# A fused attention and two-layer feed-forward kernel: order of weight preparation, place of the result sums, and where the first quad's products stand

## The chip, the core and the metric

The kernel runs on one core of a Trainium2 chip. The time is device microseconds of one execution, the median of several; smaller is better. Engines are called by their names or as the profile abbreviates them: TensorE (PE, its weight loads PEld), VectorE (DVE), ScalarE (ACT), GpSimd (POOL) and SyncE (SP), which issues nearly all DMAs.

## The reference

```python
# q, k, v: (4, 8, 576, 64), s: (4, 8, 576)
cum  = cumsum(maximum(s, 0), -1)
bias = -(cum[..., :, None] - cum[..., None, :])
scores = where(causal, -1e9, scale * q @ k.T + minimum(bias, 0))
x = (softmax(scores) @ v), heads joined             # (2304, 512)
h = x @ moe_w_in;   g = maximum(0.01 * h, h)         # 512 -> 2048
x = g @ moe_w_out                                    # 2048 -> 512
h = x @ moe2_w_in;  g = maximum(h, 0) + log1p(exp(-abs(h)))
out = g @ moe2_w_out                                 # (2304, 512)
```

The weights arrive as 64-bit floats.

## The kernel before

**Numbers in two parts.** Every matmul operand is a pair of rounded tiles, high and low, and each product is three matmuls (high by high, high by low, low by high). ScalarE rounds a tile to its high part, GpSimd (or VectorE) subtracts to get the low part.

**Stages.** Attention ends near 247 us. The first feed-forward layer goes through 68 steps: four groups of four blocks of 128 hidden units, in a group the token chunks (512, 512, 256, 512, 512 tokens; two of 384 in the first group), for each chunk the four blocks. Step n issues `h_mm` (12 matmuls) for itself and, `LAG` = 3 steps late, `out_mm(n-3)` (12 matmuls). At the fourth block of a chunk VectorE adds four PSUM banks to `acc` (L861). Five banks take turns for these sums, so the next chunk's first `out_mm` needs the adds of the last chunk. ScalarE makes `gf` (`leaky`, L834), and a step later `g_parts` makes `gh` on ScalarE and `gl` on GpSimd (L151).

**Weights on the way.** A block of 64-bit weights is loaded raw by SyncE (`load_w`, L93 for the first matrix, L98 for the second; 512 KB) into one of two raw buffers, one step before ScalarE reads it. `split_w` turns a block of the first layer into a pair: Abs and Copy on ScalarE, four steps on VectorE (L114, L117, L120, and the integer add L123), Copy on ScalarE, subtraction on GpSimd (L133). `prepare` does the same for the 32 blocks of the second layer, adds the sums of quarter blocks that a seven-product block scheme (Strassen-Winograd) needs, and `stage` (L705) writes high and low parts back to DRAM as `w2d`: the two `move`s (L713, L714) stand next to each other in SyncE's queue, and the second one needs GpSimd's result. `at(n, ...)` puts work into step n, `later(n, ...)` into a tick n steps on, `plan` holds it. Each engine works its queue strictly in the order in which the code issues.

**Second layer.** 16 quads (2 pairs of token chunks, 8 double blocks). A quad's seven products go into four banks X, Y, K, Z (L1026); VectorE adds the products into results in SBUF (`join`, L1038); for each of four results a `Unit` computes maximum(h, 0) + log1p(exp(-abs(h))): four ACT steps, `value` (L978) and `rest` (L981) on VectorE, `correct` (L984) and `low` (L992) on GpSimd. Then eight output sums (L1075) that VectorE adds to `acc` (L1081 for the first, L1083). The 256 tokens between the pairs go the plain way (`Plain`, L1102). `on(t, ...)` gives every piece a time; pieces are issued in order of these times, about 1.36 us of TensorE to a unit. The operands `B11`, `T1` to `T4`, `B21`, `B22` of the quads are sums of quarters of `acc` (`combine`, `x_high`, `x_low`).

## Time and profile before

| what | us |
|---|---|
| median of 3 runs | 975.86 (974.29 to 975.87) |
| the profiled execution, its own time | 974.51 |
| span in its profile | 972.7 |
| busy: TensorE | 952.0 (98%) |
| busy: VectorE, ScalarE, GpSimd | 714.9, 576.6, 532.2 |

The page divides the span into the busy time of each engine; matmuls overlap, so the busy sum of TensorE says little on gaps. Those are read from the starts of consecutive matmuls in the timeline, and from the view of waits, which says which instruction released a waiting one.

### The profile page before, as it was taken

How to read it: one execution, taken by the hardware profiler on the slowest of the kernel's cores; microseconds unless marked ns; L12 is line 12 of the kernel's file. 1: busy time of each engine (PE TensorE's matmuls, PEld its weight loads, DVE VectorE, ACT ScalarE, POOL GpSimd, SP SyncE). 2: the span in 40 equal slices, each digit the busy share in tenths (PEclk: the TensorE clock that was granted, in tenths of full speed). 3: DMA queues.
4: the chain of work that ended last, by engine and by line, in shares of the span. 5: the costliest groups of instructions: out<-in, count | busy, mean ns of one | idle time of the engine just before them, and what ended most of it. 6: DMA issues, size and time to landing. Idle time of an engine off the chain costs nothing.

```text
span 972.7 us, 15423 instructions
## 1 busy us (share of the span) xinstructions
PE 952.0 (98%) x5173; PEld 767.4 (79%) x5173; DVE 714.9 (73%) x1326; ACT 576.6 (59%) x1185; POOL 532.2 (55%) x516
## 2 busy tenths in 40 slices
PE   9999999999999989998999999999999999999998
PEld 6666777777988868886888888788888778888786
DVE  7888667553368778996877725787779887887777
ACT  6888667564565455555554525765566675555562
POOL 7788556452356576756755422755445454555443
PEclk9999999999999999999999999999999999999999
DMA  7444442411636566556686133242425248345302
GB/s 243 143 160 145 128 144 98 149 61 47 227 105 218 168 192 206 186 185 201 197 272 232 49 130 130 92 133 74 160 64 172 87 144 309 132 134 170 131 0 87
DMA packets 79251, 143.61 MB, mean 148 GB/s; under 512 B 7626, under 2 KB 24906, under 8 KB 79172
## 3 DMA queue, kind: packets, MB, share of 16 engines
q1 hardware_dynamic: 78740, 141.87, 44.3%
q8 instruction: 41, 0.67, 0.3%
q10 hardware_dynamic: 432, 0.75, 0.2%
q14 instruction: 38, 0.31, 0.1%
HBM read 109.33 MB, written 33.25 MB: 147 GB/s over the span
## 4 chain that ended last, share of the span: by engine, by line
PE 69%; DVE 8%; POOL 7%; issue 5%; DMA 5%; ACT 5%; SPq 1%; POOLq 0%; DVEq 0%; ACTq 0%
PE ps_out L1075 15%; PE ps_h L145 13%; PE ps_h L1026 13%; PE ps_out L854 9%; PE pt_s L316 4%; PE pt_t L377 3%; PE ps_o L635 3%; PE pt_v L409 3%; PE ps_h L1102 2%; DMA rawi<-in_moe_w_in 2%; POOL stg L712 2%; DMA rawo<-in_moe_w_out 2%; POOL l L984 1%; PE pt_s L409 1%; POOL gl L992 1%
## 5 line engine op out<-in xcount | busy, mean ns | idle before, releaser
L984 POOL TENSOR_TENSOR l<-l,v 128x512 f32<-128x512 f32 x72 | 94.6, 1314 | 140.0 <-DVE v L981 134.9
L151 POOL TENSOR_TENSOR gl<-gf,gh 128x512 fp32r<-128x512 f32 (+2 forms) x68 | 91.1, 1341 | 115.3 <-ACT gh L150 65.9
L360 POOL TENSOR_SCALAR sc<-sc,st 128x512 f32<-128x512 f32 (+4 forms) x160 | 88.4, 563 | 79.3 <-DVE st L356 61.5
L992 POOL TENSOR_TENSOR gl<-l,gh 128x512 fp32r<-128x512 f32 x72 | 95.3, 1324 | 53.6 <-ACT gh L988 53.6
L145 PE MATMUL ps_h<-xh,wih 128*128 128x512 f32 (+2 forms) x320 | 120.4, 376 | 0.0
L145 PE MATMUL ps_h<-xl,wih 128*128 128x512 f32 (+2 forms) x320 | 118.4, 370 | 0.0
L145 PE MATMUL ps_h<-xh,wil 128*128 128x512 f32 (+2 forms) x320 | 118.3, 370 | 0.0
L1075 PE MATMUL ps_out<-woh,gh 128*128 128x512 f32 x290 | 113.4, 391 | 2.2 <-DVE acc L1081 1.4
L1075 PE MATMUL ps_out<-wol,gh 128*128 128x512 f32 x290 | 112.5, 388 | 0.0
L988 ACT ACTIVATE gh<-l 128x512 fp32r<-128x512 f32 x72 | 45.6, 633 | 108.6 <-POOL l L984 108.4
L854 PE MATMUL ps_out<-gh,woh 128*128 128x512 f32 (+2 forms) x272 | 100.6, 370 | 6.5 <-DVE acc L861 6.5
L349 ACT ACTIVATE sc<-sc,st 128x512 f32<-128x512 f32 (+2 forms) x144 | 83.4, 581 | 34.7 <-DVE st L337 28.8
L854 PE MATMUL ps_out<-gl,woh 128*128 128x512 f32 (+2 forms) x272 | 100.1, 368 | 2.2 <-POOL gl L151 2.2
L1083 DVE TENSOR_TENSOR acc<-ps_out,acc 128x512 f32<-128x512 f32 (+1 forms) x127 | 85.6, 678 | 19.8 <-PE ps_out L1075 18.8
L854 PE MATMUL ps_out<-gh,wol 128*128 128x512 f32 (+2 forms) x272 | 99.9, 367 | 0.0
L1026 PE MATMUL ps_h<-xh,wih 128*128 128x512 f32 x224 | 89.1, 398 | 0.8 <-DVE u L1038 0.7
L1075 PE MATMUL ps_out<-woh,gl 128*128 128x512 f32 x290 | 88.9, 388 | 0.0
L1038 DVE TENSOR_TENSOR u<-ps_h,u 128x512 f32<-128x512 f32 x80 | 55.1, 688 | 44.3 <-PE ps_h L1026 30.8
L1026 PE MATMUL ps_h<-xl,wih 128*128 128x512 f32 x224 | 87.4, 390 | 0.0
L1026 PE MATMUL ps_h<-xh,wil 128*128 128x512 f32 x224 | 87.2, 389 | 0.0
L834 ACT ACTIVATE gf<-ps_h 128x512 f32<-128x512 f32 (+2 forms) x68 | 36.7, 540 | 62.7 <-PE ps_h L145 52.8
L981 DVE SCALAR_TENSOR_TENSOR v<-v,e 128x512 f32<-128x512 f32 x72 | 73.7, 1024 | 0.0
(169 smaller groups left out, 2361.9 us busy)
## 6 DMA issues: line engine op xcount, KB each, us to landing
w2d<-stg SPq DMA_DIRECT2D x88, 256.0 KB
rawi<-in_moe_w_in SPq DMA_DIRECT2D x32, 512.0 KB
rawo<-in_moe_w_out SPq DMA_DIRECT2D x32, 512.0 KB
wih<-w2d SPq DMA_DIRECT2D x64, 256.0 KB
wil<-w2d SPq DMA_DIRECT2D x64, 256.0 KB
woh<-w2d SPq DMA_DIRECT2D x32, 256.0 KB
wol<-w2d SPq DMA_DIRECT2D x32, 256.0 KB
K<-in_k SPq DMA_DIRECT2D x15, 432.0 KB
```

The source lines that it names most:

```text
L145: nc.tensor.matmul(ps, a, b, start=kk == 0 and n == 0, stop=kk == KD - 1 and n == 2)
L151: nc.gpsimd.tensor_tensor(gl, gf, gh.bitcast(F32), op=ALU.subtract)
L349: nc.scalar.activation(x, x, AF.Exp, scale=-1.0, bias=self.stat(0, e + self.last), accum_out=self.stat(1, e))
L360: nc.gpsimd.tensor_scalar(x, x, self.stat(2, e), 1.0, op0=ALU.mult, op1=ALU.mult)
L854: nc.tensor.matmul(ps, a, b, start=f == 0 and m == 0, stop=f == G - 1 and m == 2)
L981: nc.vector.scalar_tensor_tensor(self.t, self.t, -1.0, self.e, op0=ALU.add, op1=ALU.subtract)
L984: nc.gpsimd.tensor_tensor(self.l, self.l, self.t, op=ALU.subtract)
L992: nc.gpsimd.tensor_tensor(self.gl, self.l, self.gh.bitcast(F32), op=ALU.subtract)
L1026: nc.tensor.matmul(self.ps[name], x, y, start=n < 4 and kp == 0 and m == 0, stop=kp == 1 and m == 2, skip_group_check=n >= 4,)
L1038: nc.vector.tensor_tensor(self.u[out], self.ps[bank], self.u[other], op=ALU.add)
L1075: nc.tensor.matmul(u, a, v, start=m == 0, stop=m == len(ops) - 1)
L1083: nc.vector.tensor_tensor(d[..., w], o[..., w], d[..., w], op=ALU.add)
```

## The change

The change has three parts, and SBUF moves between them.

1. **Preparation of weights.** The second weight pool is gone until the second layer (six buffers of each kind instead of eight). Raw buffers are four instead of two, and a raw block is loaded two steps ahead. All 32 `prepare` blocks use one ring of four `ws` tiles, `stage` has six `stg` buffers instead of four. 22 of the 32 blocks are spread over groups 1 and 2, ten over the first 13 steps of group 3. The move of the low part is issued one tick after that of the high part. The add for second-matrix blocks of the first layer goes from VectorE to GpSimd. `g_parts` goes to the front of its tick.
2. **Sums in PSUM.** Joins write into the banks Y, K and Z themselves, e + 1 goes into one PSUM bank `v` (a tile in SBUF for the first quad), and `rest` writes over e. Z is one bank for all quads. Units start every 2.6 instead of 2.1 units of time, `high` and `low` come later in them. T1 and T2 overwrite B11 in `acc`, and some `x_low` go to GpSimd.
3. **First quad.** Its seven products are issued before the last three `out_mm` of the first layer, its operands are made over more steps, and its first-matrix weights are fetched at step 18 of the last group.

```diff
 def split_w(layer, f, nm, at):
-        wp = wpools[(layer * NF + f) % (2 * G) // 6]
+        wp = wpools[0]
         def add():
-            wio.get("add", nc.gpsimd).tensor_tensor(m, m, t, op=ALU.add)
+            wio["add"][nm].tensor_tensor(m, m, t, op=ALU.add)
...
-    wio["i"] = wio["o"] = enter(0, "raw", bufs=2)
-    wio["add"] = nc.vector
+    wio["i"] = wio["o"] = enter(0, "raw", bufs=4)
+    wio["add"] = {"i": nc.vector, "o": nc.gpsimd}
...
 def stage(j, k, src, own=False):
-        hi = tpool.tile([P, DM], F32R, tag="stg", name="stg", bufs=4)
+        hi = prep.tile([P, DM], F32R, tag="stg", name="stg", bufs=6)
...
             move(w2d[j, k], hi)
-            move(w2d[j, k + 1], lo)
+            later(1, move, w2d[j, k + 1], lo)
...
 def prepare(n, j, e, nm):
-        if nm == "i":
-            m = tpool.tile([P, DM], I32, tag="ws", name="ws", bufs=2)
-        else:
-            m = wio["tmp"].tile([P, DM], I32, tag="wm", name="wm")
+        m = prep.tile([P, DM], I32, tag="ws", name="ws", bufs=4)
...
 def leaky(n, N, ps):
-        later(1, parts)
+        todo.setdefault(clock[0] + 1, []).insert(0, (parts, ()))
...
+        own = (2, 5, 8, 11, 15, 18, 16, 19) if g > 1 else (None,) * 4 + (3, 6, 4, 7)
+        for j, n in enumerate(own):
+            if n is not None:
+                at(max(a + n - 2, 0), load_w, *w)
+                at(a + n, split_w, *w, (1, 1, 1, 1, 2, 2))
...
+    spare = [[n for n in r if n not in taken] for r in (range(a, z), range(z, z + 13))]
+    spare = [r[k * len(r) // m] for r, m in zip(spare, (22, 10)) for k in range(m)]
+    for n, x in zip(spare, blocks):
+        at(max(n - 2, 0), load_w, 1, 2 * x[0] + x[1], x[2])
+        at(n, prepare, n, *x)
...
-    at(begin[NG - 1] + 2, fetch, 0, 0, "i")
+    at(begin[NG - 1] + 18, fetch, 0, 0, "i")
...
+    for nm, n in (("B11", k), ("T1", k + 2), ("T3", k + 4), ("B21", k + 5), ("T2", k + 6), ("T4", z - 1), ("B22", z)):
+            at(m, x_low, 0, nm, kp, nc.gpsimd if nm in ("T3", "B21") else nc.vector)
...
-    for n in range(len(steps) - LAG, len(steps)):
-        tick()
-        out_mm(n)
...
+    Z = psA.tile([P, 512], F32, tag="s1", name="ps_h", bufs=2)
+    bank_v = []
...
         def total(self):
-            self.t = tpool.tile([P, 512], F32, tag="v", name="v")
-            nc.scalar.activation(self.t, self.e, AF.Identity, bias=1.0)
+            nc.scalar.activation(self.v(), self.e, AF.Identity, bias=1.0)
         def rest(self):
-            nc.vector.scalar_tensor_tensor(self.t, self.t, -1.0, self.e, op0=ALU.add, op1=ALU.subtract)
+            nc.vector.scalar_tensor_tensor(self.e, self.v(), -1.0, self.e, op0=ALU.add, op1=ALU.subtract)
...
-            free[0] = b + 2.1
+            free[0] = b + gap
-                (1.4, self.value), (1.85, self.rest), (2.4, self.correct), (3.5, self.high), (4.0, self.low),
+                (1.4, self.value), (1.85, self.rest), (2.4, self.correct), (gap + 1.5, self.high), (gap + 2.9, self.low),
...
+            if name not in self.ps:
+                tag, bufs = next(banks["ps_h"]) if self.first_one else TAGS[name]
...
-            on(t + 3.05, self.join, "C22", "K", "C12")
-            on(t + 4.05, self.join, "C22", "Z", "C22")
+            on(t + 3.05, self.join, "K", 2, 3)
+            on(t + 4.05, self.join, "Z", 3, "Y")
...
-        if n:
+        if n == 0:
+            for i in range(LAG, 0, -1):
+                on(t, out_mm, len(steps) - i)
+                t += 2
+        else:
             quads[n - 1].outputs(t)
```

What this does to SyncE's queue near the middle of group 1: `stg` and `ss` rows are moves to `w2d`, those that wait for Activation carry a high part, those that wait for Pool a low part; `rawi` and `rawo` rows are loads. Before:

```order
L82 DMA w2d_3162<-stg_4011 128x512 [waits Activation_49]
L82 DMA w2d_3162<-ss_3912 128x512 [waits DMAHW5_49,Pool_49]
L82 DMA w2d_3162<-stg_4015 128x512 [waits DMAHW6_49,Activation_49]
L82 DMA w2d_3162<-stg_4059 128x512 [waits Pool_49]
L93 DMA rawi_4065<-in_moe2_w_in 128x4x256 [waits DMAHW0_49,DVE_49]
```

Now, at the same kind of block:

```order
L93 DMA rawi_3966<-in_moe2_w_in 128x4x256 [waits DMAHW4_49,DVE_49]
L82 DMA w2d_3162<-ss_3818 128x512 [waits DMAHW5_49,Pool_49]
L82 DMA w2d_3162<-stg_3962 128x512 [waits DMAHW6_49,Activation_49]
L82 DMA w2d_3162<-stg_3972 128x512 [waits DMAHW7_49,Activation_49]
L93 DMA rawi_4024<-in_moe2_w_in 128x4x256 [waits DMAHW0_49,DVE_49]
L82 DMA w2d_3162<-stg_4008 128x512 [waits DMAHW1_49,Pool_49]
```

The low part of a tile no longer stands right behind its high part; the load behind it is for a block two steps ahead.

GpSimd's queue in the middle of group 1, at the chunk of 256 tokens: `gl` is the low part of a step's activations, `wil` and `wol` those of first-layer weights, `stg` and `ss` those of second-layer weights. Before:

```order
L712 TENSOR_TENSOR stg_5071<-wm_4966,stg_5027 128x512 [waits DMAHW2_49,Pool_49]
L133 TENSOR_TENSOR wil_5110<-wm_5015,wih_5108 128x512 [waits Activation_49]
L712 TENSOR_TENSOR stg_5112<-ws_4920,stg_5069 128x512 [waits DMAHW5_49,DMAHW4_49,DMAHW6_49,DMAHW0_49,Pool_49]
L151 TENSOR_TENSOR gl_5117<-gf_5075,gh_5116 128x512 [waits PE_49,Activation_49]
L151 TENSOR_TENSOR gl_5160<-gf_5124,gh_5159 128x512 [waits PE_49,Activation_49]
```

Now:

```order
L151 TENSOR_TENSOR gl_5046<-gf_5000,gh_5045 128x256 [waits PE_49,Activation_49,Pool_49]
L123 TENSOR_TENSOR wm_5002<-wm_5002,wt_5003 128x512 [waits DVE_49]
L712 TENSOR_TENSOR ss_4911<-ss_4911,stg_5010 128x512 [waits DMAHW5_49]
L712 TENSOR_TENSOR stg_5058<-ws_4954,stg_5014 128x512 [waits DMAHW7_49,Pool_49]
L151 TENSOR_TENSOR gl_5095<-gf_5061,gh_5094 128x512 [waits PE_49,Activation_49]
L133 TENSOR_TENSOR wol_5100<-wm_5002,woh_5098 128x512 [waits Activation_49]
```

`gl` stands ahead of the other work of its tick, and the add (L123) has come from VectorE and waits for it.

VectorE's queue where the layers meet: L861 before and L853 now are the adds of the first layer's last chunk. Before (the banks 6427, 6434, 6451, 6459 are X, Y, K, Z of the first quad):

```order
L861 TENSOR_TENSOR acc_3149<-ps_out_6344,acc_3149 128x512
L861 TENSOR_TENSOR acc_3149<-ps_out_6345,acc_3149 128x512
L1038 TENSOR_TENSOR u_6449<-ps_h_6434,u_6449 128x512
L1038 TENSOR_TENSOR u_6466<-ps_h_6451,u_6449 128x512
L1038 TENSOR_TENSOR u_6466<-ps_h_6459,u_6466 128x512
L1038 TENSOR_TENSOR u_6508<-ps_h_6451,u_6449 128x512
L978 SCALAR_TENSOR_TENSOR l_6506<-ps_h_6427,l_6506 128x512
```

Now (X, Y, K, Z are 6386, 6393, 6410, 6369):

```order
L958 SCALAR_TENSOR_TENSOR l_6472<-ps_h_6410,l_6472 128x512
L961 SCALAR_TENSOR_TENSOR e_6469<-v_6451,e_6469 128x512
L853 TENSOR_TENSOR acc_3149<-ps_out_6338,acc_3149 128x512
L853 TENSOR_TENSOR acc_3149<-ps_out_6339,acc_3149 128x512
L853 TENSOR_TENSOR acc_3149<-ps_out_6340,acc_3149 128x512
L853 TENSOR_TENSOR acc_3149<-ps_out_6341,acc_3149 128x512
L958 SCALAR_TENSOR_TENSOR l_6529<-ps_h_6393,l_6529 128x512
```

The four adds have moved from ahead of the quad's first join to between the units of K and Y.

## Rows read from the trace of the kernel before

**Rows 1.** Page, part 1: span; engine, busy us, share of the span, instructions.

```profile
span 972.7 us, 15423 instructions
...
PE 952.0 (98%) x5173; PEld 767.4 (79%) x5173; DVE 714.9 (73%) x1326; ACT 576.6 (59%) x1185; POOL 532.2 (55%) x516
```

**Rows 2.** TensorE in order of time: start us, duration us, engine, line, instruction, shape.

```profile
559.80 0.39 PE L854 MATMUL ps_out<-gh,woh 128*128 128x512 f32 x1
...
586.77 0.39 PE L854 MATMUL ps_out<-gl,woh 128*128 128x512 f32 x1
587.27 0.50 PE L1026 MATMUL ps_h<-xh,wih 128*128 128x512 f32 x1
...
968.71 0.40 PE L1075 MATMUL ps_out<-woh,gl 128*128 128x256 f32 x2
```

**Rows 3.** Waits of TensorE: us in total, times, longest us.

```profile
PE ps_out L854 <- DVE acc L861: 6.5, 3, 3.0
PE ps_out L854 <- POOL gl L151: 2.2, 3, 1.0
PE ps_out L1075 <- DVE acc L1081: 1.4, 2, 1.0
```

**Rows 4.** TensorE in order of time at two stalls.

```profile
344.42 0.39 PE L854 MATMUL ps_out<-gh,wol 128*128 128x512 f32 x1
345.78 0.50 PE L854 MATMUL ps_out<-gl,woh 128*128 128x512 f32 x1 [0.98 <-POOL gl L151]
349.25 0.80 PE L854 MATMUL ps_out<-gh,woh 128*128 128x512 f32 x1 [2.97 <-DVE acc L861]
...
353.00 0.39 PE L145 MATMUL ps_h<-xh,wih 128*128 128x512 f32 x1
...
449.22 0.39 PE L854 MATMUL ps_out<-gh,wol 128*128 128x512 f32 x1
...
453.62 0.50 PE L854 MATMUL ps_out<-gh,woh 128*128 128x512 f32 x1 [2.97 <-DVE acc L861]
...
458.53 0.39 PE L145 MATMUL ps_h<-xh,wil 128*128 128x512 f32 x1
```

**Rows 5.** Other engines in order of time before the first of them.

```profile
340.23 4.61 SPq L82 DMA_DIRECT2D w2d<-stg  x2
...
344.17 0.66 ACT L731 ACTIVATE ws<-rawi 128x512 f32<-128x512 f32 x1 [2.09 <-DMA rawi<-in_moe_w_in]
...
344.86 1.15 DVE L735 TENSOR_SCALAR ws<-ws 128x512 f32<-128x512 f32 x1 [1.52 <-ACT ws L731]
...
348.79 1.41 DVE L861 TENSOR_TENSOR acc<-ps_out,acc 128x256 f32<-128x256 f32 x4
```

**Rows 6.** Waits of SyncE's queue, 270 to 500 us.

```profile
SPq L82 <- POOL stg L712: 74.7, 27, 4.8
```

**Rows 7.** VectorE in order of time, 614 to 623 us.

```profile
616.76 1.50 DVE L978 SCALAR_TENSOR_TENSOR l<-u,l 128x512 f32<-128x512 f32 x1 [0.85 <-ACT l L971]
...
618.79 1.51 DVE L981 SCALAR_TENSOR_TENSOR v<-v,e 128x512 f32<-128x512 f32 x1
```

**Rows 8.** Groups by shape, VectorE, 247 to 973 us: busy us, mean ns.

```profile
L981 DVE SCALAR_TENSOR_TENSOR v<-v,e 128x512 f32<-128x512 f32 x72 | 73.7, 1024 | 0.0
L978 DVE SCALAR_TENSOR_TENSOR l<-u,l 128x512 f32<-128x512 f32 x48 | 61.5, 1281 | 3.7 <-ACT l L971 3.7
...
L978 DVE SCALAR_TENSOR_TENSOR l<-ps_h,l 128x512 f32<-128x512 f32 x24 | 16.5, 687 | 6.1 <-ACT l L971 5.7 <-issue 0.3
```

**Rows 9.** Groups by shape, GpSimd: the add, where it ran there.

```profile
L123 POOL TENSOR_TENSOR wm<-wm,wt 128x512 int32<-128x512 int32 x12 | 15.7, 1309 | 0.0
```

**Rows 10.** By stretch: PE, PEld, DVE, ACT, POOL busy; clock; DMA share, GB/s.

```profile
349.40:352.40 3.00, 3.00 (x7) 2.33 (x8) 2.79 (x7) 2.31 (x5) 1.71 (x2) 0.50 0.50 115
376.00:418.00 42.00, 42.00 (x187) 34.80 (x186) 37.38 (x45) 23.81 (x43) 27.52 (x18) 1.00 0.63 201
838.00:880.00 42.00, 42.00 (x183) 33.90 (x184) 33.95 (x43) 24.64 (x42) 21.19 (x17) 1.00 0.48 150
```

More of the change, by code (lines that the diff above doesn't have):

```diff
@@ L82, in move @@
         queue.dma_start(dst.bitcast(F32), src.bitcast(F32))
-    wt, wio = {}, {}
+    wt, wio = {}, {"add": {"i": nc.gpsimd, "o": nc.gpsimd}}
     wpools = [ctx.enter_context(pool("wpool0", bufs=6))]
@@ L870, in attn_moe_moe @@
     for g in range(1, NG):
-        a, z = begin[g - 1], begin[g]
-        when = [(a + n - 1, a + n) for n in (0, 3, 6, 8, 11, 14, 16, 19)] if g > 1 else [None] * 4 + [(0, 2), (1, 4), (3, 6), (5, 8)]
-        for j, x in enumerate(when):
-            if x:
-                f, nm = divmod(j, 2)
-                w = (0, g * G + f, "io"[nm])
-                at(x[0], load_w, *w)
-                at(x[1], split_w, *w, (1, 1, 1, 1, 2, 2))
-                taken.add(x[1])
-    free = [n for n in range(begin[1], len(steps)) if n not in taken]
@@ L881, in attn_moe_moe @@
-    for j in range(NJ):
-        for e, nm in ((0, "i"), (1, "i"), (0, "o"), (1, "o")):
-            n = free.pop(0)
-            at(n - 1, load_w, 1, 2 * j + e, nm)
-            at(n, prepare, n, j, e, nm)
+        a = begin[g - 1]
+        own = (2, 5, 8, 11, 15, 18, 16, 19) if g > 1 else (None,) * 4 + (3, 6, 4, 7)
+        for j, n in enumerate(own):
+            if n is not None:
+                w = (0, g * G + j // 2, "io"[j % 2])
+                at(max(a + n - 2, 0), load_w, *w)
+                at(a + n, split_w, *w, (1, 1, 1, 1, 2, 2))
+                taken.add(a + n)
@@ L886, in attn_moe_moe @@
+    blocks = [(j, e, nm) for j in range(NJ) for e, nm in ((0, "i"), (1, "i"), (0, "o"), (1, "o"))]
+    a, z = begin[1], begin[NG - 1]
+    spare = [[n for n in r if n not in taken] for r in (range(a, z), range(z, z + 13))]
[3 more added lines that the diff above has]
+        at(n, prepare, n, *x)
     for c in range(B - 1):
         at(2 * c + 2, load_acc, c)
-    at(begin[NG - 1] + 2, fetch, 0, 0, "i")
+    at(begin[NG - 1] + 18, fetch, 0, 0, "i")
@@ L889, in attn_moe_moe @@
     at(begin[NG - 1] + 4, fetch, 0, 0, "o")
     k = begin[NG - 1, chunks[1]] + G + LAG
-    for kp in range(2):
-        at(k, combine, 0, "T1", kp)
-        at(k, x_high, 0, "B11", kp)
-        at(k, x_low, 0, "B11", kp)
-        at(k + 1, combine, 0, "T3", kp)
-        at(k + 1, x_high, 0, "T1", kp)
-        at(k + 1, x_low, 0, "T1", kp)
-        at(k + 2, combine, 0, "T2", kp)
-        at(k + 2, x_high, 0, "T3", kp)
-        at(k + 2, x_low, 0, "T3", kp)
-        at(k + 3, x_high, 0, "T2", kp)
-        at(k + 3, x_low, 0, "T2", kp)
-        z = begin[NG - 1, chunks[3]] + G - 1
-        at(z, x_high, 0, "B21", kp)
-        at(z, x_low, 0, "B21", kp)
-        at(z + 1, combine, 0, "T4", kp)
-        at(z + 1, x_high, 0, "T4", kp)
-        at(z + 1, x_low, 0, "T4", kp)
-        at(len(steps) - 1, x_high, 0, "B22", kp)
-        at(len(steps) - 1, x_low, 0, "B22", kp)
+    z = len(steps) - 1
@@ new lines, in attn_moe_moe @@
+    follow = {"B11": "T1", "T1": "T3", "T3": "T2"}
+    for nm, n in (("B11", k), ("T1", k + 2), ("T3", k + 4), ("B21", k + 5), ("T2", k + 6), ("T4", z - 1), ("B22", z)):
+        for kp in range(2):
+            m = min(n + kp, z)
+            if nm == "T4":
+                at(m, combine, 0, nm, kp)
+            at(m, x_high, 0, nm, kp)
+            at(m, x_low, 0, nm, kp, nc.gpsimd if nm in ("T3", "B21") else nc.vector)
+            if nm in follow:
+                at(m, combine, 0, follow[nm], kp)
@@ L927, in attn_moe_moe @@
             out_mm(n - LAG)
[L928 to L930 removed]
     flush()
     stages[0].close()
[L935 to L936 removed]
+    wpools.append(enter(1, "wpool1", bufs=2))
+    lpool = enter(1, "lpool", bufs=3, side="right")
+    gpools = [enter(1, "gpool1", bufs=3, side="right"), gpool]
+    order = [0]
     events = []
@@ L1031, in first, with join @@
         def first(self):
-            self.u["C12"] = sum_tile()
-            nc.scalar.activation(self.u["C12"], self.ps["X"], AF.Copy)
-        def join(self, out, bank, other):
-            if out not in self.u:
-                self.u[out] = sum_tile()
-            nc.vector.tensor_tensor(self.u[out], self.ps[bank], self.u[other], op=ALU.add)
+            self.u[2] = wio["tmp"].tile([P, 512], F32, tag="wm", name="u")
+            nc.scalar.activation(self.u[2], self.ps["X"], AF.Copy)
+        def join(self, bank, old, new):
+            b = self.ps[bank]
+            if new == 3:
+                self.u[3] = wio["tmp"].tile([P, 512], F32, tag="wt", name="u")
+            if new in (2, 3):
+                o = self.u[new]
+            else:
+                o = self.ps[new]
+            nc.vector.tensor_tensor(o, b, self.u[old], op=ALU.add)
         def at(self, t):
+            gap = 2.3 if (self.sb, self.j) == (1, NJ - 1) else 2.6
             for n, nm in enumerate("XYKZXKZ"):
```

93 lines of the change are left out of this document (43 added, 50 removed).

## The prediction

> **What bounds the kernel now.** I read the page's first part first: TensorE is busy for 952.0 of 972.7 us [rows 1]. So nothing can be won that is not an idle gap of TensorE, or slow matmuls after one. No matmul is added or taken away. The second view is TensorE in order of time, for the undisturbed spacing: from 559.80 to 586.77 us there are 119 intervals between matmuls of 512 columns, 0.2266 us each [rows 2]. With this spacing every longer interval is lost time.
>
> In the first layer two places stand out [rows 4]. From 344.42 to 353.00 there are 11 intervals, 2.49 us at the undisturbed spacing, so 6.1 of the 8.58 us are lost. From 449.22 to 458.53 there are 16 intervals, 3.63 us, so 5.7 of 9.31 are lost. Each has a wait of 2.97 us for the adds to `acc`, most of the 6.5 us that the view of waits puts down to them [rows 3]; a smaller wait for `gl` stands ahead of it. [...] Smaller gaps, the rest of the waits for the adds and for `gl` with the slow start behind each, come to some 2.3 us (near 327 and 537 us). I put the first layer at 14 us lost.
>
> The second layer starts at 587.27 and its last matmuls at 968.71, 381.4 us [rows 2]. By the code it has 16 quads of 42 products, 16 of 48 output matmuls and 96 plain output matmuls, 12 of which count as halves: 1530 of 512 columns and 204 of 256. At 0.2266 and, for the halves, 0.12 us (an estimate: half and a little overhead) that is 371.2. So about 10 us are lost, in many small pieces, the largest being waits on VectorE's copies to `acc` [rows 3]. Together some 24 us are within reach, and 950 us would be a kernel without gaps.
>
> **Why it stalls.** Before the first stall, SyncE's two moves to `w2d` take from 340.23 for 4.61 us, since the low part's waits for GpSimd, and the raw load behind them gets out only then. ScalarE waits 2.09 us for a raw block (344.17), VectorE 1.52 us for ScalarE (344.86), and the four adds that free the banks stand behind that in VectorE's queue and start at 348.79 [rows 5]. The moves' waits for GpSimd come to 74.7 us in 27 cases between 270 and 500 us [rows 6]. In the second layer the view of VectorE shows `value` at 1.50 and `rest` at 1.51 us where copies to `acc` stand in between [rows 7]. `value` takes 1281 ns with its operand in SBUF and 687 ns with it in PSUM, `rest` 1024 ns with both in SBUF [rows 8].
>
> **The change, part by part.** *Preparation.* The low part's move goes out a tick later, when GpSimd has had a step for it; a raw block is asked for two steps ahead, into four buffers; `gl` leads its tick on GpSimd. This takes away what started both stalls, and the small wait for `gl` ahead of them. What is late next is VectorE itself, 37.4 of 42 us busy [rows 10]: at the 256-token chunk a converted block and four adds meet within a step of some 4 us. Ten adds fewer on VectorE help. On GpSimd an add costs 1.31 us [rows 9], four per group, beside 27.5 of 42 us busy [rows 10], with no path of its own. I leave 0.8 us per group, 2.5 us in all, as lost: bounds are 0 (no gap) and 8 (one stall of 6.1 and small gaps). Gain 11.5 us. The number of operations and DMAs stays the same. The smaller weight ring costs nothing: each block of the next group is ready one step or more before it is used, and its buffer's last reader has been issued by then. The fetch of the first quad's eight first-matrix tiles (2.1 MB) moves from step 2 to 18 on SyncE, past all preparation moves. Its last buffers are free after the matmuls of step 17, five half steps of 2.72 us (12 x 0.2266) ahead of the first product, and 13.6 us at the 150 to 201 GB/s of the rows [rows 10] move 2.0 to 2.7 MB; half of it can go earlier. So I take zero, upper bound 3 us.
>
> *Where the layers meet.* Before, the first product follows the last `out_mm` at 0.50 instead of 0.23 us [rows 2]: 0.3 us. Now the seven products (9.5 us) stand ahead of the last three `out_mm` (8.2 us). The operands of the first product are done by step 12; the last, B22, has about 8 us of products ahead of it. But VectorE's queue now has the four adds of the last `out_mm` ahead of `value` for the bank Y of the first quad, and the first plain products take that bank's place. The fourth add can begin only when TensorE has finished `out_mm`, and takes about 0.69 us, as does `value` after it (both read PSUM) [rows 8], and 0.2 for the start: TensorE waits about 1.7 us instead of going on. [...] Net with the 0.3 it is a loss of 1.4 us.
>
> *Sums in PSUM.* 48 `value`s go from 1281 to 687 ns, 28.5 us; 68 `rest`s read PSUM instead of SBUF, by the same rows about 0.34 us less each, 23 us. So VectorE has some 50 us less to do, of 385. Joins and `total`, with PSUM as output, have no row; I take the time with PSUM as input (0.69) as lower, 1.28 as upper bound, and the lower as the likelier, since every form with PSUM stays near it. None of this is on TensorE's path but the copies to `acc` behind it, where the waits are. A wait is added: one bank Z for all quads, which the next quad's fourth product needs. Per quad (20.8 us in the second half) ScalarE has 21 instructions, 24.64 us for 42 [rows 10], thus 12.3 us. Its first unit can start after the fifth product, 6.8 us into the quad, so the last unit's `value` comes some 19 to 20 us in; the next quad's fourth product begins at 20.4 + 4.1 = 24.5 us. Four to five microseconds of slack hide it, and `v` is free again after each `rest`. Of the 10 us lost in small pieces I leave 3.7, those that hang on products and not on VectorE's length: gain 6.3, bounds 2 and 9. Low parts of operands on GpSimd, ten of about 1.3 us, are hidden (21.2 of 42 us busy) [rows 10].
>
> [...]
>
> **The sum.** 11.5 - 1.4 + 6.3 = 16.4 us. From the profiled execution's 974.51 us this gives 958.1. That execution lies 1.35 us under the median of the runs and within their range; I add 0.9 and forecast **959.0**.
>
> **Rivals.**
> *VectorE stays the bound in the first layer.* With 37.4 of 42 us busy the adds may still come late once, one stall of 6.1 us: 959 + 6 = 965. For it: the same work on VectorE in the same steps. Against it: its queue waited for raw blocks, not only for its own work.
> *PSUM brings VectorE nothing.* The 687 ns may hold only where `value` met no GpSimd work; then the second layer keeps its 10 us, 959 + 6 = 965. Against it: 24 `value`s, one in every quad and plain piece, have that mean [rows 8]. [...]
> *Slower: the add on GpSimd closes a ring.* VectorE's third step, GpSimd's add, ScalarE's Copy and its Prelu wait for one another in strict queues. If the add came so late that `gl` behind it missed its `out_mm` two steps later, each case would cost a stall of 5.9 us as measured [rows 4]. There are ten such blocks; from three on (16.4/5.9 = 2.8) the gain is gone, and with four it is 959 + 4 x 5.9 = 983. Against it: two steps are over 8 us, and GpSimd's longest hold of SyncE was 4.8 us [rows 6].
> *The change doesn't do what it says*: the raw loads still wait behind moves, both stalls remain, and the second layer gains no more than the place where the layers meet loses: about 975.
>
> **How the numbers follow.** Forecast, 954 to 964: 0.61. Nearly no gap left, 951 to 954: 0.08. One stall kept, 964 to 970: 0.14. PSUM brings nothing, about 965: 0.05. Nothing changes: 0.05. The ring: 0.07. A measurement of this kernel can tell about 0.2% (2 us) from no change. Faster by more: 0.61 + 0.08 + 0.14 + 0.05 = 0.88; within: 0.05; slower: 0.07. The range 953 to 969 leaves out the last two, most of the 0.08 and a little of the 0.14.
>
> **What would show it.** Right: the 2.97 us waits for `acc` are gone near 345 and 450 us, the clock stays at 1.00 there, SyncE's waits for GpSimd fall far below 74.7 us, all `value`s stand near 690 ns, and one wait of 1 to 2 us precedes the first plain products. Wrong: waits of ScalarE for GpSimd's add with gaps behind them, a wait of the fourth product for the bank Z, or of the first product for its weights.

## Result and the profile after

The changed kernel takes 961.29 us (median, 960.88 to 961.56) beside 975.67 for the kernel before on the same chip: ratio 0.9855, 95% interval 0.9838 to 0.9872. Forecast were 959.0 us and a range of 953 to 969. The gain is 14.4 us, 2.3 less than the 16.7 that lie between 959.0 and 975.67.

The page of after, part 1 (span; engine, busy us, share of the span, instructions), answers to [rows 1]:

```profile
span 959.8 us, 15357 instructions
...
PE 945.1 (98%) x5173; PEld 767.8 (80%) x5173; DVE 672.5 (70%) x1306; ACT 574.7 (60%) x1185; POOL 553.2 (58%) x536
```

VectorE has 42 us less to do, GpSimd 21 us more; TensorE has the same 5173 matmuls. So as forecast the gain lies in TensorE's gaps. I measure them as the prediction did, over all starts of matmuls: every interval above the undisturbed spacing (0.227 us for 512 columns, 0.173 for 384, 0.12 for 256) counts as lost, matmuls at the lower clock included. From the first layer's first product to 589 us the kernel before lost 14.9 us and the changed one loses 7.0; from there on it was 10.0 and is 4.4. Together that is 13.5 us less, where the two profiled executions (974.51 and 961.56) lie 12.95 apart: the first layer began 0.8 us later in the second one (244.08 against 243.28), and the ends make up the rest.

TensorE's waits in the changed kernel (us in total, times, longest us), to be held against [rows 3]:

```profile
PE ps_out L846 <- DVE acc L853: 4.1, 2, 2.9
PE ps_out L1068 <- DVE acc L1076: 1.7, 2, 1.4
PE ps_h L1013 <- DVE ps_h L1030: 0.8, 1, 0.8
```

The waits for GpSimd's `gl` are gone, and of the two stalls of [rows 4] the first is gone too: 0.4 us are lost near 344. The second stands. TensorE in order of time at it, and where the layers meet:

```profile
443.28 0.39 PE L846 MATMUL ps_out<-gl,woh 128*128 128x512 f32 x1
446.54 0.80 PE L846 MATMUL ps_out<-gh,woh 128*128 128x512 f32 x1 [2.87 <-DVE acc L853]
...
589.59 0.39 PE L846 MATMUL ps_out<-gl,woh 128*128 128x512 f32 x1
589.82 0.28 PE L1095 MATMUL ps_h<-xh,wih 128*128 128x256 f32 x1
```

The wait of 2.87 us for an add to `acc` is the 2.97 of before; with the slow matmuls behind it some 4.5 us are lost here, and 1.5 us at a wait of 1.27 near 546 us. Where the layers meet there is no gap at all: the first plain product starts 0.23 us after the last output matmul.

What the adds waited for shows VectorE's own queue (start us, duration us, line, tiles) ahead of that stall, and GpSimd's beside it:

```profile
433.81 1.26 DVE L732 TENSOR_SCALAR ws<-ws 128x512 f32<-128x512 f32 x1 [0.88 <-ACT ws L728]
435.11 1.40 DVE L733 TENSOR_SCALAR ws<-ws 128x512 int32<-128x512 int32 x1
436.54 1.67 DVE L734 SCALAR_TENSOR_TENSOR ws<-rawo,ws 128x512 int32<-128x512 int32 x1
438.35 1.56 DVE L735 CUSTOM_DVE_ANT_0 ws<-ws,wt 128x1024 uint16<-128x1024 uint16 x1
439.84 1.52 DVE L732 TENSOR_SCALAR ws<-ws 128x512 f32<-128x512 f32 x1
...
444.62 1.53 DVE L735 CUSTOM_DVE_ANT_0 ws<-ws,wt 128x1024 uint16<-128x1024 uint16 x1
446.08 1.40 DVE L853 TENSOR_TENSOR acc<-ps_out,acc 128x256 f32<-128x256 f32 x4
447.41 0.41 DVE L732 TENSOR_SCALAR ws<-ws 128x512 f32<-128x512 f32 x1
```

```profile
437.62 1.75 POOL L151 TENSOR_TENSOR gl<-gf,gh 128x512 fp32r<-128x512 f32 x1
439.33 1.75 POOL L133 TENSOR_TENSOR wol<-wm,woh 128x512 fp32r<-128x512 f32 x1
...
443.90 1.71 POOL L712 TENSOR_TENSOR stg<-ws,stg 128x512 fp32r<-128x512 f32 x1
447.42 1.55 POOL L151 TENSOR_TENSOR gl<-gf,gh 128x512 fp32r<-128x512 f32 x1 [1.81 <-ACT gh L150]
```

Two conversions of a block (L732 to L735) stand ahead of the four adds, and they take 6.0 and 6.2 us, while GpSimd works beside them without a break until 445.61: L732 takes 1.26 and 1.52 us here, and 0.41 at 447.41, where GpSimd has been idle for 1.81 us and starts again at 447.42. The adds begin at 446.08, though TensorE had gone on from the chunk's last product at 440.1.

In the second layer VectorE's groups by shape (line, tiles, count, busy us, mean ns, idle before), 600 to 940 us, answer to [rows 8]:

```profile
L958 DVE SCALAR_TENSOR_TENSOR l<-ps_h,l 128x512 f32<-128x512 f32 x65 | 44.4, 683 | 4.3 <-POOL xl L801 2.5 <-ACT l L952 1.4 <-POOL gl L974 0.3
L961 DVE SCALAR_TENSOR_TENSOR e<-ps_v,e 128x512 f32<-128x512 f32 x65 | 44.2, 679 | 0.0
L1030 DVE TENSOR_TENSOR ps_h<-ps_h,u 128x512 f32<-128x512 f32 x44 | 30.6, 695 | 35.0 <-PE ps_h L1013 34.9
```

`value` (L958) is at 683 ns everywhere, `rest` (L961) fell from 1024 to 679, and a join that writes PSUM takes 695. What is left of lost time in this layer lies all between 756 and 786 us.

### The profile page after: what moved, and what is told of

Read it like the earlier page. It is cut to its first block, busy times and chain, and to the rows that moved or that the text cites. A ratio compares the mean times of both kernels' runs of the same rounds, so it can differ in the third digit from the quotient of the medians.

```text
span 959.8 us, 15357 instructions
## 1 busy us (share of the span) xinstructions
PE 945.1 (98%) x5173; PEld 767.8 (80%) x5173; DVE 672.5 (70%) x1306; ACT 574.7 (60%) x1185; POOL 553.2 (58%) x536
## 4 chain that ended last, share of the span: by engine, by line
PE 77%; DVE 12%; POOL 4%; issue 3%; ACT 2%; DMA 1%; SPq 0%; DVEq 0%; POOLq 0%; ACTq 0%
PE ps_out L1068 18%; PE ps_h L145 15%; PE ps_h L1013 14%; PE ps_out L846 12%; PE pt_s L316 4%; PE pt_t L377 3%; PE ps_o L635 3%; PE pt_v L409 3%; PE ps_h L1095 2%; DVE ws L734 2%; PE pt_s L409 1%; DVE ws L733 1%; DVE ws L732 1%; DVE acc L853 1%; POOL l L964 1%
## 5 line engine op out<-in xcount | busy, mean ns | idle before, releaser
L964 POOL TENSOR_TENSOR l<-l,e 128x512 f32<-128x512 f32 x72 | 94.4, 1311 | 173.4 <-DVE e L961 160.0
L151 POOL TENSOR_TENSOR gl<-gf,gh 128x512 fp32r<-128x512 f32 (+2 forms) x68 | 88.6, 1304 | 123.2 <-ACT gh L150 82.6
L1076 DVE TENSOR_TENSOR acc<-ps_out,acc 128x512 f32<-128x512 f32 (+1 forms) x127 | 86.7, 684 | 46.2 <-PE ps_out L1068 44.0
L337 DVE CUSTOM_DVE_ANT_0 sc<-pt_s,mask 128x512 f32<-128x512 f32 (+3 forms) x129 | 59.1, 482 | 16.4 <-PE pt_t L377 15.4
L145 PEld LDWEIGHTS ps_h<-xh,wil 128*128 128x128 f32 x320 | 60.2, 188 | 9.6
```

What stands on the lines that cost most here:

```text
L145: nc.tensor.matmul(ps, a, b, start=kk == 0 and n == 0, stop=kk == KD - 1 and n == 2)
L151: nc.gpsimd.tensor_tensor(gl, gf, gh.bitcast(F32), op=ALU.subtract)
L337: nc.vector.tensor_tensor_reduce(out=self.sc[:, j, c], in0=self.ps[j][:, c], in1=m, scale=-scale, scalar=low, op0=ALU.add, op1=ALU.min, ac ...
L964: nc.gpsimd.tensor_tensor(self.l, self.l, self.e, op=ALU.subtract)
L1076: nc.vector.tensor_tensor(d[..., w], o[..., w], d[..., w], op=ALU.add)
```

## Experiments

Lost time in the two layers, measured as above, tells the runs apart better than the medians, since it leaves out the attention stage, whose end moved by up to 0.9 us between runs. It is read from one profiled execution of each kernel, and what the clock behind a single wait added to it differed by up to 3 us between these runs (last section). The kernel before had medians of 975.67 to 976.44 beside them; ratios are to those.

| run | median us | ratio, 95% interval | lost, first layer | lost, second |
|---|---|---|---|---|
| before | 975.67 | 1 | 14.9 | 10.0 |
| changed | 961.29 | 0.9855 (0.9838 to 0.9872) | 7.0 | 4.4 |
| e1 loads one step ahead | 960.7 | 0.9842 (0.9829 to 0.9856) | 7.0 | 4.4 |
| e2 moves together | 961.0 | 0.9841 (0.9827 to 0.9854) | 7.2 | 4.4 |
| e3 split at the end | 960.51 | 0.9842 (0.9829 to 0.9856) | 5.5 | 4.3 |
| e4 add on VectorE | 959.64 | 0.9832 (0.9818 to 0.9845) | 6.0 | 4.3 |
| e5 five edits undone | 962.07 | 0.9845 (0.9821 to 0.9868) | 7.8 | 4.4 |
| e6 no block at step 13 | 955.85 | 0.9781 (0.9758 to 0.9804) | 2.1 | 4.3 |
| e7 adds first | 954.4 | 0.9767 (0.9744 to 0.979) | 0.6 | 4.3 |
| e8 sums in SBUF | 964.24 | 0.9865 (0.9843 to 0.9887) | 7.3 | 7.0 |
| e9 e5 and buffers | 965.81 | 0.9896 (0.9883 to 0.991) | 11.5 | 4.3 |
| e10 before, own steps | 970.97 | 0.9953 (0.994 to 0.9967) | 11.0 | 9.7 |
| e11 outputs first | 965.48 | 0.9895 (0.9882 to 0.9908) | 8.4 | 8.6 |
| e12 both orders | 951.04 | 0.9744 (0.9732 to 0.9757) | 0.5 | 1.0 |

### The causes that the prediction named

**e1**: the raw loads' lead and buffers undone.

```diff
-    wio["i"] = wio["o"] = enter(0, "raw", bufs=4)
+    wio["i"] = wio["o"] = enter(0, "raw", bufs=2)
-                at(max(a + n - 2, 0), load_w, *w)
+                at(max(a + n - 1, 0), load_w, *w)
-        at(max(n - 2, 0), load_w, 1, 2 * x[0] + x[1], x[2])
+        at(n - 1, load_w, 1, 2 * x[0] + x[1], x[2])
```

> The changed kernel with the raw weights loaded one step ahead into 2 raw buffers again, instead of two steps ahead into 4; all else as changed. Theory A (the raw loads' lead is what emptied the first layer of its stalls): ScalarE's waits for raw weights come back, 25 us or more of them, and GpSimd's wait at the stalls, so most of the first layer's gain goes: 965 to 968 us. Theory B (the later move in SyncE's queue did it): within 1 us of the changed kernel's 961.3.

960.7 us, the lost time unchanged in both layers. ScalarE's waits for raw weights come back to 12.6 us only. Theory A falls for this edit by itself.

**e2**: the low part's move back in the tick of the high part's.

```diff
-            later(1, move, w2d[j, k + 1], lo)
+            move(w2d[j, k + 1], lo)
```

> The changed kernel with the low part's move to DRAM issued in the same tick as the high part's again, not a tick later. Theory A: SyncE's waits for GpSimd grow over the 70.1 us of the changed kernel, but with loads two steps ahead nothing is late: 960.8 to 961.8. Theory B (this was the step of the prediction that should free SyncE's queue): ScalarE's waits for raw weights come back and the time goes to 964 to 968.

961.0 us; 7.2 and 4.4 us lost. Nor was it this move by itself (theory B). It didn't even do on SyncE's queue what I had named as its sign: between 270 and 500 us the queue waits for GpSimd's low parts nearly as long as before the change ([rows 6]: 74.7 us; 77.0 in e2). The changed kernel:

```profile
SPq L82 <- POOL stg L712: 70.1, 30, 3.9
```

**e3**: the activations' split back at the end of its tick.

```diff
-        todo.setdefault(clock[0] + 1, []).insert(0, (parts, ()))
+        later(1, parts)
```

> The changed kernel with the split of a step's activations at the end of its tick again, not at its head. Theory A: GpSimd's low part of an activation was late for want of its place in the tick; 0.98 and 0.54 and 0.70 us of TensorE's waits for it come back: 962.5 to 964. Rival: it was late only because ScalarE, ahead of it, stood waiting for a raw load, and that is gone: within 0.3 of 961.3.

960.51 us, no wait for `gl`: in this kernel it is not late for its place in the tick. The wait at 443 us is the same (2.89 us); that only 5.5 us are lost comes from the clock, 1.00 behind the wait where the changed kernel had 0.50 (last section).

**e4**: the adds of out-weights in the first layer back on VectorE. There are ten of them; the expectation says eight.

```diff
-    wio["add"] = {"i": nc.vector, "o": nc.gpsimd}
+    wio["add"] = {"i": nc.vector, "o": nc.vector}
```

> The changed kernel with the add of the first layer's out weights on VectorE again instead of on GpSimd (8 adds in the first layer). If VectorE is simply the engine with too much work there, 8 adds of about 0.7 to 1.2 us come back on it and the stall at 443 us grows by 0.7 to 1.6 us: 962 to 963. Theory C (GpSimd's instruction costs VectorE as much as it saves, since VectorE's instructions take about twice as long beside it): within 0.5 of 961.3, or faster by up to 1.

959.64 us, somewhat faster than expected; the medians' difference to the changed kernel is within what can be told, but the wait at the second stall fell from 2.9 to 1.9 us. So this piece of the change worked, if anything, against it, which fits theory C. What the add by itself does to VectorE's instructions was not shown: in the changed kernel the clamp L732 at 433.81 us, beside such an add (433.48 us, 1.31 us long), took 1.26 us, but in e4 the same clamp, at 432.13, took 1.51 without it.

**e5**: all of these undone at once, and the second layer's blocks on the first 32 free steps.

```diff
-    spare = [[n for n in r if n not in taken] for r in (range(a, z), range(z, z + 13))]
-    spare = [r[k * len(r) // m] for r, m in zip(spare, (22, 10)) for k in range(m)]
+    spare = [n for n in range(a, len(steps)) if n not in taken]
```

> The changed kernel with five of its edits to the first layer undone together: raw loads one step ahead into 2 buffers, the low part's move in the high part's tick, the activations' split at the end of a tick, the out weights' add on VectorE, and the second layer's 32 blocks on the first 32 free steps instead of spread over 22 and 10. What stays as changed: the steps at which the first layer's own weights are split, its ring of 6, and the 6 and 4 buffers for staged and prepared blocks. Theory A2 (each of these edits alone is enough to empty the first stall, so undoing one showed nothing): most of the first layer's 7.9 us come back, 965 to 969. Theory P (it is the steps of the split, which this kernel keeps, or the added staging buffers): within 1.5 of the changed kernel's 961.3.

962.07 us; 7.8 us lost in the first layer, so all five together are worth 0.8 us there. ScalarE's waits for raw weights in the first layer (us in total, times, longest) are all back:

```profile
ACT ws L728 <- DMA rawo<-in_moe_w_out: 24.9, 11, 5.1
ACT ws L728 <- DMA rawi<-in_moe_w_in: 18.7, 12, 3.8
ACT wm L108 <- DMA rawo<-in_moe_w_out: 14.5, 7, 5.0
ACT wm L108 <- DMA rawi<-in_moe_w_in: 9.1, 4, 4.2
```

That is 67.2 us of the very wait that [rows 5] show ahead of the first stall (2.09 us), one of up to 5.1 us. But the 0.8 us is a difference of two stalls that go opposite ways. The first stall is back, and the chain of [rows 5] stands ahead of it again. ScalarE, VectorE and TensorE at it:

```profile
341.21 0.67 ACT L728 ACTIVATE ws<-rawi 128x512 f32<-128x512 f32 x1 [2.02 <-DMA rawi<-in_moe_w_in]
341.98 0.43 DVE L732 TENSOR_SCALAR ws<-ws 128x512 f32<-128x512 f32 x1 [1.54 <-ACT ws L728]
345.30 1.41 DVE L853 TENSOR_TENSOR acc<-ps_out,acc 128x256 f32<-128x256 f32 x4
345.77 0.50 PE L846 MATMUL ps_out<-gh,woh 128*128 128x512 f32 x1 [1.81 <-DVE acc L853]
```

Here 3.7 us are lost, where the changed kernel loses 0.4. The second stall is shorter: a wait of 1.80 us instead of 2.87, and 2.1 us lost instead of 4.5. None of e1 to e4 brings the first stall back alone. Nor can it be the blocks: by the code both kernels prepare the same blocks at the same steps up to the first stall, and differ from step 17 of that group on. So at the first stall theory A2 holds, in that more than one of the loads' lead, the move, the split's place and the add must be undone before the stall comes back. Which of them it takes was not tried.

### What emptied the first stall

**e9**: e5, with the buffers for prepared and staged blocks undone too (`stg` 4 instead of 6 besides).

```diff
-        m = prep.tile([P, DM], I32, tag="ws", name="ws", bufs=4)
+        if nm == "i":
+            m = prep.tile([P, DM], I32, tag="ws", name="ws", bufs=2)
+        else:
+            m = wio["tmp"].tile([P, DM], I32, tag="wm", name="wm")
```

> The kernel of e5 (five edits to the first layer undone together, 962.1) with the buffers for prepared and staged blocks undone as well: 2 buffers for in-weights, the out-weights in the 2 temporaries that the first layer's own weights use, and 4 for staged blocks. What then remains as changed in the first layer is the steps at which its own weights are split, and their ring of 6. Theory P1 (ScalarE and VectorE were held up by GpSimd's release of those shared temporaries: ScalarE waited 3.29 us for GpSimd's subtraction right ahead of the first stall): the first layer's loss goes from 7.8 back to about 14 us, 967 to 970. Theory P2 (the steps of the split decide): the loss stays at 7 to 9 us, 961 to 964.

965.81 us, 11.5 us lost: between the two theories. The buffers are worth 3.7 us in the layer.

**e10**: the kernel before with only the steps of the first layer's own weights changed (and of the blocks, which take what is free).

```diff
-        when = [(a + n - 1, a + n) for n in (0, 3, 6, 8, 11, 14, 16, 19)] if g > 1 else [None] * 4 + [(0, 2), (1, 4), (3, 6), (5, 8)]
+        when = [(a + n - 1, a + n) for n in (2, 5, 8, 11, 15, 18, 16, 19)] if g > 1 else [None] * 4 + [(1, 3), (4, 6), (2, 4), (5, 7)]
```

> The kernel before, with one edit: the first layer's own weights are split at the changed kernel's steps (2, 5, 8, 11, 15, 18, 16, 19 of a group of 20 instead of 0, 3, 6, 8, 11, 14, 16, 19; 3, 6, 4, 7 in the first group), and with that the blocks of the second layer stand on the steps that this leaves free. Theory P2: the first layer's loss falls from 14.9 to 7 to 9 us: 967 to 970. Theory P1: it stays within 2 us, 974 to 977.

970.97 us, 11.0 us lost: again between. The steps are worth 3.9 us in the layer, and TensorE's waits for `gl` are gone with them alone. The sums of the layer fit together: from before, steps 3.9 (14.9 to 11.0), buffers 3.7 (11.5 to 7.8), the other five edits 0.8 (7.8 to 7.0), with 0.5 between 11.0 and 11.5 for what else differs. By place they read otherwise (us lost):

| run | first stall, 341 to 365 us | second stall, 440 to 465 us | rest of the first layer |
|---|---|---|---|
| before | 6.1 | 5.7 | 3.1 |
| e10, before with the own steps | 3.9 | 2.0 | 5.1 |
| e9, changed without the five edits and the buffers | 3.9 | 3.7 | 3.9 |
| e5, changed without the five edits | 3.7 | 2.1 | 2.0 |
| changed | 0.4 | 4.5 | 2.1 |

The own steps took 2.2 us off the first stall, the buffers next to nothing, and the edits of e5 3.3 us. What the buffers are worth lies elsewhere: 1.3 us near 430 us, and 1.6 at the second stall, where e9 and e5 both wait for 1.80 us and only the spacing of the matmuls behind the wait differs (in e9 0.42 to 0.43 us from 452.5 to 455.5 us, in e5 0.22 to 0.24). Which of the buffers did it, those of prepared or of staged blocks, wasn't tried apart.

### What is left

**e6**: no block prepared at step 13 of a group.

```diff
-    spare = [[n for n in r if n not in taken] for r in (range(a, z), range(z, z + 13))]
+    spare = [[n for n in r if n not in taken and n not in (a + 13, a + 33)] for r in (range(a, z), range(z, z + 13))]
```

> The changed kernel with no block of the second layer's weights prepared at step 13 of a group of 20, and the free step 17 used in its place. Theory C (what is left at 443 us is the four adds of the 256-token chunk standing on VectorE behind two conversions of 6.0 and 6.2 us, of which this takes one out of the way): the 3.0 us gap at 443 and the lower clock behind it (about 4.7 us together) go or fall under 1: 956.5 to 958. Rival (VectorE is full throughout the layer, and what is late is late wherever the blocks stand): the gap comes back elsewhere in the layer, within 1 of 961.3.

955.85 us, a little under the range expected: the gap at 443 is gone, the one near 546 (operands of the second layer, not a block) stays. By the code the blocks of steps 13 and 14 of two groups stand at 14 and 17 now, all others as before. Theory C holds, the rival falls.

**e7**: where a 256-token chunk's last output step is due, it is written ahead of that tick's work.

```diff
+        early = n >= LAG and steps[n - LAG][0] > 0 and steps[n - LAG][2] == G - 1 and steps[n - LAG][1][1] < 512
+        if early:
+            out_mm(n - LAG)
         tick()
...
-        if n >= LAG:
+        if n >= LAG and not early:
             out_mm(n - LAG)
```

> The changed kernel with the output products and adds of the 256-token chunk's last step written ahead of that tick's work, so that VectorE's four adds stand ahead of the conversion of that tick instead of behind it; TensorE's order and all places are as changed. Theory C: the adds come about 5 us sooner, the gaps at 443 (3.0 and the clock behind it) and 546 us (1.4) go: 955.5 to 957.5. Rival (VectorE is full, a conversion that is pushed back makes the next step's adds or parts late): one gap goes and another of 2 to 5 us comes, 960 to 963.

954.4 us, under the range expected and faster than the changed kernel by 6.9; 0.6 us lost in the first layer, with no interval over 0.02 us too long, so that this is rounding. VectorE in order of time at the former stall:

```profile
437.32 1.57 DVE L735 CUSTOM_DVE_ANT_0 ws<-ws,wt 128x1024 uint16<-128x1024 uint16 x1
438.81 1.41 DVE L853 TENSOR_TENSOR acc<-ps_out,acc 128x256 f32<-128x256 f32 x4
440.13 1.45 DVE L732 TENSOR_SCALAR ws<-ws 128x512 f32<-128x512 f32 x1
```

The four adds come 7.3 us sooner than at 446.08 (0.6 of that because the layer began sooner), and the conversion that stood ahead of them comes after; VectorE does the same work (678.2 us busy in the whole run, after 672.5), and nothing behind it is late. It was the place in the queue, not the load. The adds take 1.41 us for the four, the same as at 446.08, although GpSimd is busy beside them here and was idle there (445.61 to 447.42):

```profile
438.80:440.20 1.40, 1.40 (x9) 1.20 (x8) 1.40 (x6) 1.28 (x3) 1.40 (x2) 1.00 0.88 282
```

(stretch, us; busy PE, PEld, DVE, ACT, POOL; clock, DMA share, GB/s.) So beside GpSimd these adds, with one operand in PSUM, took no longer than without it; the clamp L732, with its operands in SBUF, took 1.45 us right behind them at 440.13 and 0.42 at 445.45, where GpSimd was idle (444.16 to 446.81).

### The second layer

**e8**: sums and e + 1 back in SBUF, orders kept.

```diff
-        def __init__(self, fetch_h, fetch_v=total_bank):
+        def __init__(self, fetch_h, fetch_v=total_tile):
...
-                o = self.ps[new]
+                o = self.u[new] = lpool.tile([P, 512], F32, tag="u", name="u", bufs=4)
```

(`total_tile` gives one SBUF tile to all units, and units K, Y, Z read `u`.)

> The changed kernel with the second layer's result sums and e + 1 in SBUF again (4 buffers for sums, 1 for e + 1), all orders as changed. Theory D (VectorE's instructions with an operand in PSUM are what shortened the second layer): value and rest go from about 680 ns back to 1000 to 1280 ns, the waits of TensorE for sums and adds come back: 963 to 967. Rival (the gain is from the order of the second layer's work, VectorE has room there): instructions longer, but the time within 1 of 961.3.

964.24 us. VectorE's groups, 600 to 940 us:

```profile
L968 DVE SCALAR_TENSOR_TENSOR e<-v,e 128x512 f32<-128x512 f32 x64 | 57.8, 903 | 0.0
...
L965 DVE SCALAR_TENSOR_TENSOR l<-u,l 128x512 f32<-128x512 f32 x43 | 45.4, 1057 | 0.0
L965 DVE SCALAR_TENSOR_TENSOR l<-ps_h,l 128x512 f32<-128x512 f32 x22 | 15.2, 691 | 8.8 <-POOL gl L981 4.8 <-POOL xl L801 2.5 <-ACT l L959 1.5
```

With SBUF operands the instructions are longer by 220 to 370 ns (903 and 1057 against 679 and 683), and the lost time rises from 4.4 to 7.0 us. So PSUM is worth 2.6 us of this layer's 5.6. The other 3.0 are the remainder and were not undone in a run of their own; what is left to cause them is the new order of the layer's work (units 2.6 products apart, operands over more steps, low parts on GpSimd).

**e11**: the last three output steps ahead of the first quad's products again.

```diff
-                on(t, out_mm, len(steps) - i)
-                t += 2
+                on(-0.5 - 0.1 * i, out_mm, len(steps) - i)
```

> The changed kernel with the first layer's last three output steps ahead of the first quad's seven products again, all else as changed. By the prediction's step (first plain products wait 1.7 us with the new order, 0.3 with the old) the time would fall by 1.4 to 959.9; the changed kernel's trace has no gap there, so the rival is that the order covers something: the plain products or the first quad's units then wait for VectorE, and the time rises by 0.3 to 2 us, 961.6 to 963.3. No more than 0.3 either way if neither holds.

Written so, the second quad's fourth product goes into the shared bank Z before the first quad's last unit has read it, so that this unit works on other data; matmuls and their sizes are the same. 965.48 us, over both ranges expected. TensorE where the plain products follow the first quad, and VectorE's `value` that it waits for:

```profile
590.45 0.39 PE L1013 MATMUL ps_h<-xh,wil 128*128 128x512 f32 x1
593.25 0.39 PE L1095 MATMUL ps_h<-xh,wih 128*128 128x256 f32 x1 [2.41 <-DVE l L958]
```

```profile
592.50 0.69 DVE L958 SCALAR_TENSOR_TENSOR l<-ps_h,l 128x512 f32<-128x512 f32 x1 [0.43 <-ACT l L952]
```

593.19 is the end of the second unit's `value`, that of K. So the plain products take K's bank, and in the changed kernel the three output steps (8.2 us of matmuls) stand where TensorE would wait for it. With this kernel's banks and units the order is worth up to 4 us (2.6 at this wait, 1.0 for `gl` near 612 and 0.5 behind both); the first layer's 1.4 us more come from slow matmuls behind the wait at 443 us, outside the edit (last section).

**e12**: e7, with two moves at the end of the second layer's operands.

```diff
-                on(b + n - 0.9, combine, 1, nm, kp)
-            on(b + n, x_high, 1, nm, kp)
-            on(b + n + 0.8, x_low, 1, nm, kp, nc.gpsimd if nm in ("T3", "B21", "B22") else nc.vector)
+                on(b + n - 0.9 + (1.5 if nm == "T4" else 0), combine, 1, nm, kp)
+            n += 1.5 if nm == "T4" else 0
+            on(b + n, x_high, 1, nm, kp)
+            on(b + n + (0.9 if nm == "T1" else 0.8), x_low, 1, nm, kp, nc.gpsimd if nm in ("T3", "B21", "B22") else nc.vector)
```

The reason was in the changed kernel's VectorE (L801 and L794 make operands of the second pair, L1030 joins, L1076 adds to `acc`):

```profile
755.93 1.36 DVE L801 TENSOR_TENSOR xl<-acc,xh 128x512 fp32r<-128x512 f32 x1 [1.20 <-ACT xh L797]
757.22 0.69 DVE L1030 TENSOR_TENSOR ps_h<-ps_h,u 128x512 f32<-128x512 f32 x1
...
774.57 1.76 DVE L794 TENSOR_TENSOR acc<-acc 128x512 f32<-128x512 f32 x1 [1.85 <-POOL xl L801]
776.25 0.68 DVE L1076 TENSOR_TENSOR acc<-ps_out,acc 128x512 f32<-128x512 f32 x1
```

VectorE stood idle for ScalarE (1.20 us) and for GpSimd (1.85 us) with the join and the add behind it that TensorE wanted.

> The kernel of e7 (adds of the 256-token chunk ahead of that tick's work, 954.4) with two more moves in the second layer's one stretch with gaps: the low part of T1 right behind the join that TensorE waits for at 757 us instead of right ahead of it, and T4's combination, high and low part 1.5 products later, so that VectorE no longer stands waiting for GpSimd at 773 us with the add that TensorE wants behind it. Theory C (what TensorE waits for is late by its place in VectorE's queue, not by VectorE's load): the gaps of 0.98 and 1.6 us go, 951.5 to 952.7. Rival (they are late by load): 953.7 to 955.

951.04 us (950.78 to 951.14), a little under the range expected, 24.9 less than before and 10.3 less than the changed kernel. All that its view of TensorE's waits shows from 240 us on is:

```profile
PE ps_out L1071 <- DVE acc L1079: 0.3, 1, 0.3
```

## Why the prediction was right, and where it was not

*What bounds the kernel, and the sum.* TensorE's gaps were the right account: 13.5 us of lost time less, 12.95 us in the executions, where I had 16.4. The total is closer than its parts: preparation brought 3.9 us less than forecast and the sums 0.7 less, while the place where the layers meet came out 1.7 better. That the last makes up for part of the others is luck.

*Preparation.* This is the term that was mis-sized: 2.5 us to be left, 7.0 measured, so 7.6 us of gain instead of 11.5 (of the 7.9 in the table 0.3 belong to the place where the layers meet). The step that failed is "I leave 0.8 us per group": at the 256-token chunk one group lost 4.5 us and another 1.5. I had named what is late there, a converted block and four adds, as "late next", and also as a rival ("one stall kept"). The rival's price was about right, 4.5 for 6.1, but its reason, VectorE's load, was not: e7 leaves the load and has no stall. It is four adds behind two conversions, which take 6 us each beside GpSimd; no wait for a raw load stands ahead of them.

The sentence "This takes away what started both stalls" was half right. For the first stall it stands as a bundle: 0.4 us are left, and with the edits undone together the chain of [rows 5] and 3.7 us are back (e5). No single one of the three is needed for it (e1, e2, e3). But 2.2 of the stall's 6.1 us went by the steps of the own weights (e10), which I had passed over, and the second stall has the other cause. The buffers, which I had counted at nothing, are worth 3.7 us in the layer (e9), none of it at the first stall.

*Ten adds fewer on VectorE* I counted as a help; e4 shows a shorter wait with them back.

*Where the layers meet.* Forecast 1.7 us (its terms, 0.69, 0.69 and 0.2, make 1.6, and no row shows the 0.2: from the end of VectorE's instruction to the matmul it released e11 shows 0.06 us, 593.19 to 593.25, and the changed kernel 0.05, 757.91 to 757.96), measured 0. The step that failed is that the plain products take Y's bank; they take K's, whose `value` ended at 584.18 us, over 5 us ahead of them. The four adds do stand between K and Y, from 587.98 to 590.7 us, as the order shows. The wait is real where the output steps don't cover it: 2.41 us in e11.

*Sums in PSUM.* 3.7 us forecast to be left, 4.4 measured. `value`, `rest` and joins at 679 to 695 ns, as forecast at 690; the added wait of a quad's fourth product for the bank Z never shows. But I put the whole gain of 6.3 down to PSUM; of the measured 5.6, e8 gives PSUM 2.6, and the other 3.0 are left to the order of work. That instructions with their operands in SBUF were longer in this layer is shown by e8: 903 and 1057 ns, against 679 and 683 with PSUM, means over the layer in the same order of work. Single instructions of the changed kernel show it beside GpSimd: L794, both inputs in SBUF, took 1.26 us (762.22, GpSimd busy until 762.93), and L1076, one input in PSUM, 0.68 (768.92, GpSimd busy from 768.40 to 770.14). Undisturbed both took the same, by two neighbours with GpSimd idle from 762.93 to 767.16:

```profile
764.00 0.67 DVE L794 TENSOR_TENSOR acc<-acc 128x512 f32<-128x512 f32 x1
764.60 0.68 DVE L1076 TENSOR_TENSOR acc<-ps_out,acc 128x512 f32<-128x512 f32 x1
```

*Signs.* Right: `value` near 690 ns, no wait of a fourth product for Z (the 0.8 us on the join L1030, near 758 us, is a seventh product's), no wait for GpSimd's add with a gap behind it, the 2.97 us wait near 345 gone. Wrong: the one near 450 stayed, with the lower clock behind it; no wait precedes the first plain products; and SyncE's waits for GpSimd stayed at 70.1 of 74.7. This last sign was a poor one: ScalarE's waits for raw weights are gone in the changed kernel, with SyncE's queue waiting as before.

## What to carry to other kernels

A chain of late instructions ahead of a stall says what came last, not which edit will mend it. Here any one of four edits could be undone without bringing the first stall back, and undoing them together brought back the chain and 3.7 us. The stall that was left had no late load in it at all: writing the four adds that TensorE waits for ahead of their tick's other work on VectorE was worth 6.9 us, nearly as much as the whole first part of the change. So look also at what stands ahead of the awaited instruction on its own engine, and whether it must. Where one edit is a bundle, undo its parts one by one and together before believing any of them, and compare stall by stall: over the layer e5 differs by 0.8 us only, since one stall comes back while another shrinks.
